# First attention's q and o weight gradients moved into the lead of the backward sweep, with other moves of loads, tiles and tick order

## The chip, the cores and the metric

The kernel runs on one core of a Trainium2 chip. The metric is the device time of one execution in microseconds (us). Several executions are timed, and their median is the time of a kernel. One execution more is recorded by the profiler; it has a time of its own.

## The reference

Inputs are x of 2048 tokens by 576, weights of two attentions, a gate vector and an output gradient, all bf16. The reference computes a forward pass and the gradient of everything in it:

```python
def _fwd_reference(...):                       # x is A_x; out = g*a + (1-g)*b
    g = _sigmoid((x * gate_w).sum(-1, keepdims=True))
    # A: 32 query heads of 18, one key and value head
    q = (x @ wq) as (32, 2048, 18); k = x @ wk; v = x @ wv
    a = softmax(q k^T * 18 ** -0.5) v, heads joined, @ wo
    # B: 64 segments of 32 tokens, one after the other, 32 heads of 128
    mem = mem0                                 # 8 rows
    for s in range(64):
        h = concatenate([mem, B_x of segment s])       # 40 rows
        q, k, v = h Wq, h Wk, h Wv
        p = softmax(q k^T * 128 ** -0.5, causal among the 32, memory always seen)
        o = (p v) Wo
        mem = o[:8]; outs.append(o[8:])
    b = concatenate(outs)
# returned: the output, and by jax.vjp the gradients of x, wq, wk, wv, wo,
# mem0, Wq, Wk, Wv, Wo and gate_w
```

In the kernel's list of outputs, outs[2] is the gradient of wq (x^T times dq) and outs[5] that of wo (o^T times da, where da is the gradient that reaches attention A's output and o its heads before wo). Both are sums over 2048 tokens of a 576 by 576 product.

## The kernel before, in words

Attention A and attention B share the core. B's memory makes its 64 segments a chain, forward and backward, whose steps are short and wait for each other. So the kernel runs each chain as a generator and weaves into it, step by step, another generator with A's work, which has no chain: `weave` (line 279) takes one step of the sweep per step of the chain. The stages are, in order, with their times in the profiled execution:

1. Preparation, the projections of B for all tokens, weights kept on chip or stored (0 to 440 us).
2. `b_chain_fwd` (line 333), B's forward chain over 64 segments, woven with `a_pass1`, A's forward and query-side backward pass (440 to 2135). In each segment a chain step makes q, k and v of the memory rows. `rows_copy` copies their rows and `rows_out` stores them, both through POOL's queue; `expand` (line 267) spreads probabilities over blocks on POOL.
3. `b_bulk` (line 658), the attention of B's tokens, forward and backward, for all segments (2137 to 2782). It is a software pipeline written out by hand: 16 token tiles of 8 groups of 4 heads are 128 units, and 137 ticks run over them. In each tick the list `order` says which stages are issued and how many units back each one works. `st_QT`, `st_KT`, `st_VT`, `st_GT` and `st_OT` transpose a tile on PE into a PSUM tile x_tr, of which there are two, and DVE or ACT copies it out. QT and KT carry a ride, the transposes of dS and P (x_DT and x_PT). `st_SDm` and `st_SDx` make the scores and their gradient, `st_M` masks, `st_R` sums and divides (DVE, then POOL's x_P), `st_Om` and `st_Ox` make the output, `st_Qm` and `st_Qx` the query gradient, `st_K` the memory's key and value gradients, and `B_(i)` the output projection. An engine executes its instructions in the order in which they are issued here.
4. `b_chain_bwd` (line 993), B's backward chain over 64 segments of 14 steps, woven with `a_pass2` (line 1863), the key-side sweep of A (2782 to 4388). One sweep step (the "unit") makes scores, exponentials (b_E, ACT), probabilities' gradients (b_dS, DVE) and the two accumulations for 512 columns. Its queries come in pieces of 800 columns (b_QS), one for four steps, and its keys as b_KV. SWEEP of 1024 units run here, the rest in stage 6. Twelve steps of the sweep lead, and `extra` puts 22 more into the chain's first segment.
5. `b_post` (line 1272): gradients that the chain left for later (4388 to 4604).
6. `b_dw` (line 1401): B's weight gradients, woven with the rest of the sweep, one unit for every WCOLS columns of matmul; six units come first (4604 to 5373).
7. `a_final` (line 1992): A's input gradient f_dx and A's weight gradients (5373 to the end).

Three weight tiles WT0, WT1, WT2 of 4.7 MB each (`alloc_WT`) and the output weights WoT of 4.7 MB are stored in stage 1 and 2 and loaded again for the backward chain: WT by `load_WT` in 12 pieces on SP's queue, at every fourth step from the lead's first (WT2, then WT0, then WT1), WoT by `load_WoT` on POOL's queue. Pools of SBUF are stacked: a pool opened later lies behind an earlier one, and where its tiles lie over tiles of the stage before, their first writers wait for the last readers there. Within `b_chain_bwd` the pools are rw (WoT), a3s, a3k (sweep), rs and rk, rv, rd (chain).

In stage 7 the sums for outs[2] and outs[5] are ten groups of 16 steps over token tiles, each step a matmul of 512 columns and one of 64 (PSUM tile f_big). Each group leaves through a copy f_o and a store on SP. Their operands ot and da come by `final_tok` (line 1965) at the end of stage 6.

Of the kernel before, what the change touches and what calls it, by code (L numbers as in the profile page):

```python
# [12 lines left out]
BF16 = mybir.dt.bfloat16  # L13
F32 = mybir.dt.float32
U16 = mybir.dt.uint16
U32 = mybir.dt.uint32
P = 128

D = 576
NKT = 5  # L20
# [13 lines left out]
KT_ROWS = [128, 128, 128, 128, 64]  # L34
# [1 line left out]
KR = 9  # L36
KVT = 11
KV4 = 9
SWEEP = 928
QSW = 800  # L40
WCOLS = 13312
RIDE = 24


# [6 lines left out]
class Kern:  # L51
# [224 lines left out]
    def m_rows(self, t, c):  # L276
        return t[32 * c:32 * c + 8].rearrange("p u e -> p (u e)")

    def weave(self, chain, sweep, lead, extra=(), early=None, n_early=0):
        steps = itertools.count()  # L280

        def step():
            i = next(steps)
            if i % 4 == 0 and i // 4 < n_early:
                early(i // 4)
            next(sweep, None)

        for _ in range(lead):
            step()
        extra = dict(extra)  # L290
        for i, _ in enumerate(chain):
            for _ in range(1 + extra.get(i, 0)):
                step()
        for _ in sweep:
            pass
# [37 lines left out]
    def b_chain_fwd(self, keep, sp, psum):  # L333
        nc = self.nc
# [68 lines left out]
        for s in range(NSEG):  # L403
# [79 lines left out]
            qT = sp.tile([P, 8, 4, 8], BF16, name="c_qT", bufs=1)  # L483
            nc.scalar.copy(qT[:], src)
            mT_store("k")
            rows_copy("k")
            rows_out("q")
            if s < 48:
                stash_end(*wt)
# [30 lines left out]
            proj("v", 1, (0, 1))  # L520
            yield
            proj("v", 1, (2, 3, 4))
            rows_copy("q")
            yield
            po = psum.tile([P, 8, 64], F32, name="c_x", bufs=1)
# [2 lines left out]
            for u in range(8):  # L528
                self.mm(po[:, u, 0:32], lhsT=vx[:, u, :], rhs=PBx[:, u].rearrange("p c q -> p (c q)"),
                        start=False, stop=True)  # L530
# [107 lines left out]
    def alloc_WoT(self, pool):  # L638
        self.WoT = (pool.tile([P, 4, J], BF16, name="WoT"), pool.tile([P, 4, 512], BF16, name="WoTt"))

    def load_WoT(self, pool):
        self.alloc_WoT(pool)
        for kt in range(4):
            self.nc.gpsimd.dma_start(self.WoT[0][:, kt, :], self.st_WoT[kt])
        self.nc.gpsimd.dma_start(self.WoT[1][:], self.st_WoTt[:])

    def load_blockdiag(self, t, src, tt):
        for i in range(4):
# [9 lines left out]
    def b_bulk(self, wp, lp, sp, psum):  # L658
# [243 lines left out]
        def st_K(t):  # L902
# [12 lines left out]
            if t % 4 == 3:  # L915
                c2 = t // 4 % 2
                for i in range(4):
# [1 line left out]
                    due[1].append((dst[i][:, 4 * c2:4 * c2 + 4, :], dm[32 * i:32 * i + 32].rearrange("p g w e -> p g (w e)")))  # L919

        B_ = lambda i: lambda t: st_B(t, i)
        order = [(None, st_QT), (7, B_(0)), (None, st_KT), (7, B_(1)), (4, st_Om), (5, st_OT), (7, B_(2)), (5, st_VT),
                 (7, B_(3)), (None, st_SDm), (0, st_GT), (9, st_Qm), (2, st_R), (7, st_K),
                 (None, st_SDx), (1, st_M), (4, st_Ox), (9, st_Qx)]
        done = {st_Ox: (4,), st_VT: (5,), st_SDx: (6,), st_K: (7,), st_Qx: (9,)}
        for names in (deep, ("mT", "v", "vB", "kB")):
            load(0, names)
# [62 lines left out]
        v = lambda t: t.rearrange("p (c u) d -> p c (u d)", u=8)[:, :, u * D:(u + 2) * D]  # L990
        self.nc.sync.dma_start(v(self.WT[wi][:]), v(self.st_WT[wi]))

    def b_chain_bwd(self, wot, sp, kd, kvp, keep, psum):
        nc = self.nc
        NSEG, T = self.NSEG, self.T
        self.load_WoT(wot)
        dm = [keep.tile([P, NSL, 32], BF16, name=f"dm{i}") for i in range(2)]
        hs = keep.tile([P, 2, GD], BF16, name="r_hs")
        hx = keep.tile([P, 2, 16], BF16, name="r_hx")
# [272 lines left out]
    def b_post(self, sp, rp, psum, wH):  # L1272
# [4 lines left out]
        NG = NTT * 8  # L1277
        NC = NG // 2
        pdx, C, sB, mR, T_ = {}, {}, {}, {}, {}

        def load_s(n):
            tt = NTT - 1 - n
# [10 lines left out]
        def load(c, names):  # L1293
            if c >= NC:
                return
            tt, h0 = NTT - 1 - c // 4, 8 * (c % 4)
            d = C.setdefault(c, {})
            if tt >= self.NTT - KVT:
                names = [{"q": "dk", "dO": "dv"}.get(w, w) for w in names if w != "pd"]
            for w in names:  # L1300
                if w in ("dk", "dv"):
                    d[w] = sp.tile([P, 8, P], BF16, name=f"y_l{w}", bufs=3)
                    nc.sync.dma_start(d[w][:].rearrange("p h e -> p (h e)"),
                                      self.xtok[w][tt * P:(tt + 1) * P, h0 * P:h0 * P + 1024])
                    continue
                if w == "pd":
                    d[w] = rp.tile([P, 2, 8, SEG], BF16, name="y_pd", bufs=3)
                    nc.sync.dma_start(d[w][:], self.pd_dram[tt][:, :, h0:h0 + 8, :])
                    continue
                d[w] = (rp if w == "q" else sp).tile([P, 8, P], BF16, name=f"y_{w}", bufs=3)  # L1310
                if w == "dq":
                    nc.sync.dma_start_transpose(d[w][:], self.xtok[w][tt * P:(tt + 1) * P, h0 * P:h0 * P + 1024])
                else:
                    nc.sync.dma_start(d[w][:].rearrange("p h e -> p (h e)"),
                                      self.xtok[w][tt * P:(tt + 1) * P, h0 * P:h0 * P + 1024])

        def st_KV(t):
            tt, g, r, d = NTT - 1 - t // 8, t % 8, slice(4 * (t % 2), 4 * (t % 2) + 4), C[t // 2]
            if tt >= self.NTT - KVT:
                return  # L1320
            pks = []
            for x in (1, 0):
                pk = psum.tile([P, 4, P], F32, name="y_pk", bufs=2)
                c, h2 = slice(32 * (g // 2), 32 * (g // 2) + 32), g % 2
                for i in range(4):
                    self.mm(pk[:, i, :], lhsT=sB[tt][c, i, h2, x, :], rhs=mR[tt][c, x, 4 * h2 + i, :],
                            start=True, stop=False, tp=(c.start, 0))
                pks.append(pk)
            for x, pk in zip((1, 0), pks):
                self.diag_mm(pk, d["pd"][:, x, r], d["q" if x else "dO"][:, r])  # L1330
            for w, pk in zip(("dk", "dv"), pks):
                if t % 2 == 0:
                    d[w] = sp.tile([P, 8, P], BF16, name=f"y_t{w}", bufs=2)
                nc.scalar.copy(d[w][:, r, :], pk[:])
                if t % 2 == 1:
                    h0 = 8 * (t // 2 % 4)
                    nc.gpsimd.dma_start(self.xtok[w][tt * P:(tt + 1) * P, h0 * P:h0 * P + 1024],
                                      d[w][:].rearrange("p h e -> p (h e)"))

        def st_T(t):  # L1340
            d = C[t // 2]
            T_[t] = {"dq": d["dq"][:, 4 * (t % 2):4 * (t % 2) + 4, :]}
            for w in ("dk", "dv"):
                pt = psum.tile([P, 4, P], BF16, name="y_pt", bufs=2)
                for i in range(4):
                    self.tr(pt[:, i, :], d[w][:, 4 * (t % 2) + i, :], P)
                T_[t][w] = sp.tile([P, 4, P], BF16, name="y_T", bufs=5)
                nc.vector.tensor_copy(T_[t][w][:], pt[:])
            if t % 2 == 1:
                C.pop(t // 2)  # L1350
# [15 lines left out]
                nc.gpsimd.dma_start(self.dxB_dram[tt * P:tt * P + n, :], dx[0:n, :])  # L1366

        stages = (st_KV, st_T, st_H)
        dxt = [sp.tile([P, D], BF16, name=f"y_dx{i}") for i in range(2)]
        load(0, ("pd", "q", "dO"))  # L1370
        load(0, ("dq",))
        load_s(0)
# [7 lines left out]
        for t in range(NG + len(stages) - 1):  # L1380
            if t % 3 == 2 and 0 <= t - 11 < 30:
                next(hist[(t - 11) // 15])
            if t == 16:
                for g in range(2):
                    nc.gpsimd.dma_start(
                        self.dxB_dram[T0:self.T, 288 * g:288 * g + 288].rearrange("(s r) c -> s r c", r=RIDE),
                        self.dxr_dram[0:self.NSEG - KR, 32 * g:32 * g + RIDE, :])
            for n, st in enumerate(stages):
                if 0 <= t - n < NG:
                    st(t - n)  # L1390
                if n == 0 and t == 31:
                    self.ht = self.load_h(self.db_dram, self.dm_dram, wH)
                if n == 0 and t < NG:
                    if t % 2 == 1:
                        load(t // 2 + 3, ("pd", "q", "dO"))
                    if t % 8 == 7:
                        load_s(t // 8 + 2)
                if n == 1 and t % 2 == 0 and t >= 2:
                    load(t // 2 + 2, ("dq",))

    def b_dw(self, sp, wA, wB, wH, psum, sweep):
        nc = self.nc
# [69 lines left out]
        with self.tc.manual_schedule():  # L1472
# [37 lines left out]
                nc.vector.tensor_copy(dg16[0:1, hf, :], pg[hf][0:1, 0:288])  # L1510
            nc.sync.dma_start(self.outs[11][None, :], dg16[0:1].rearrange("p a b -> p (a b)"))
            self.ftok["x"] = ht
            self.final_tok(wB, ("ot", "da"))

    def setup_A_dram(self, dram):
        T = self.T
# [475 lines left out]
    def a_final(self, sp, psum):  # L1992
# [37 lines left out]
        for kt in range(NKT):  # L2030
            drows = KT_ROWS[kt]
            cs = slice(kt * P, kt * P + drows)
            for (l, r, o) in (("x", "dq", 2), ("ot", "da", 5)):
                pw = psum.tile([P, 640], F32, name="f_big", bufs=2)
                self.row_mm(pw[0:drows], [(tok[l][:, tt, cs], tok[r][:, tt, :]) for tt in range(NTT)])
                o16 = sp.tile([P, D], BF16, name="f_o16", bufs=2)
                self.evac(o16[0:drows, :], pw[0:drows, 0:D])
                nc.sync.dma_start(self.outs[o][cs, :], o16[0:drows, :])
            pk = psum.tile([P, 4, 36], F32, name="f_pk", bufs=1)
            for tt in range(NTT):  # L2040
                self.mm(pk[0:drows, 0, :], lhsT=tok["x"][:, tt, cs], rhs=dkt[:, tt, :], start=(tt == 0),
# [7 lines left out]
def build_full(tc, A_x, A_wq, A_wk, A_wv, A_wo, B_mem0, B_Wq, B_Wk, B_Wv, B_Wo, gate_w, grad_out, outs_raw,  # L2049
# [10 lines left out]
    with SB("const") as cpool, tc.tile_pool(name="dram", bufs=1, space=bass.MemoryType.DRAM) as dram:  # L2060
# [18 lines left out]
        with ExitStack() as man:  # L2079
# [37 lines left out]
            tw = ExitStack()  # L2117
            twp = tw.enter_context(SB("tw"))
            k.alloc_WT(twp)
            with SB("rw") as rw, SB("a3s") as a3s, SB("a3k") as a3k, SB("rs") as rs, \  # L2120
                    SB("rk") as rk, SB("rv") as rv, SB("rd") as rd, PS("rp") as rp, PS("a3p") as a3p:
                k.weave(k.b_chain_bwd(rw, rs, rd, rv, rk, rp), k.a_pass2(a3k, a3s, a3p, 0, SWEEP, nc.sync, rv, 3), 12,
                        {4: 8, 7: 6, 9: 8}, k.load_WT, 12)
            wHs = ExitStack()
            wH = wHs.enter_context(SB("wH", RIGHT))
            with SB("yr", RIGHT) as yr, SB("ys") as ys, PS("yp") as yp:
# [83 lines left out]
```

## Time and profile before

| what | us |
|---|---|
| median of 3 executions | 5443.15 |
| lowest and highest | 5434.64 to 5444.33 |
| profiled execution, its time | 5478.13 |
| profiled execution, its span | 5476.4 |
| lead and first segment of the backward chain | 2782 to 2881 |
| first of the ten groups for outs[2] and outs[5] | 5424.52 |
| last DMA issue | 5465.6 |

The profile's engines are PE (matmul), PEld (its weight load, beside matmuls), DVE, ACT, POOL and SP, whose queue issues DMAs. In a row of the timeline come start, length, engine, source line, operation, output and inputs with their shapes, the count, and in brackets how long the engine was idle before and what ended that. In a row of the chain come start, length and what ran. In a row of waits: engine, who ended the wait, total us, how often, the longest. L86 is the helper through which all matmuls are issued and L91 the one for transposes, so rows are told apart by tile names. The mean granted clock of PE over the span was 0.981.

### The profile page before, as it was taken

The page shows a single profiled execution, that of the slowest core. Times are in us where ns is not written, and L with a number is a line of the kernel's source. Part 1 is how long each engine was busy: PE and PEld are TensorE (multiplying, and loading weights), DVE is VectorE, ACT ScalarE, POOL GpSimd, SP SyncE. Part 2 cuts the span into 40 slices and gives each one's busy share as a digit, 9 for nine tenths or more (in the row PEclk, how much of TensorE's full clock was granted, in tenths as well). Part 3 has the DMA queues.
Part 4 walks back from the last instruction along what each step waited for, and adds up shares of the span by engine and source line. Part 5 has one row for each costly group of instructions (what it writes and reads, how often), then busy time and mean ns, then how long its engine had stood idle before and what let it go on. Part 6 is the DMA issues. An engine that isn't in the chain of part 4 may idle for free. (4 is left out here: it accounts for less than half of the span.)

```text
span 5476.4 us, 221351 instructions
## 1 busy us (share of the span) xinstructions
PE 5171.7 (94%) x95713; PEld 2805.1 (51%) x95713; DVE 3579.9 (65%) x7083; ACT 3306.7 (60%) x4738; POOL 2163.2 (40%) x4186
## 2 busy tenths in 40 slices
PE   7999999999999998999979999999999998999998
PEld 6434444444444444766635555555555476754444
DVE  5337888888888887666658778888788822333322
ACT  4327787777777886655557777777777722222211
POOL 4004554555555544433324455455445411121113
PEclk9999999999999999999979999999999999999999
DMA  6645776666676555888874788888888878956553
GB/s 216 222 173 130 138 138 130 131 135 130 133 134 121 112 111 144 259 250 248 255 243 128 184 181 184 181 185 183 180 184 184 160 201 213 255 187 205 182 165 108
DMA packets 1048630, 959.14 MB, mean 175 GB/s; under 512 B 598882, under 2 KB 896747, under 8 KB 1038050
## 3 DMA queue, kind: packets, MB, share of 16 engines
q1 hardware_dynamic: 938434, 687.66, 54.2%
q0 software_dynamic: 100784, 247.24, 14.8%
q8 instruction: 748, 12.26, 1.0%
q10 hardware_dynamic: 8432, 10.08, 0.6%
q14 instruction: 232, 1.90, 0.1%
HBM read 522.08 MB, written 371.33 MB: 163 GB/s over the span
## 5 line engine op out<-in xcount | busy, mean ns | idle before, releaser
L1918 DVE TENSOR_TENSOR b_dS<-b_dP,b_E 128x512 bf16<-128x512 f32 x2048 | 1315.4, 684 | 533.5 <-PE b_dP L86 246.0
L1779 DVE TENSOR_TENSOR a_W<-a_dP,a_E 128x512 bf16<-128x512 f32 x2048 | 1315.7, 685 | 288.0 <-issue 131.3
L1893 ACT ACTIVATE b_E<-b_S 128x1024 bf16<-128x1024 f32 x1024 | 1048.8, 1024 | 605.2 <-PE b_dP L86 505.4
L1749 ACT ACTIVATE a_E<-a_S 128x1024 bf16<-128x1024 f32 x1024 | 1049.9, 1025 | 260.9 <-PE a_dP L86 173.4
L86 PEld LDWEIGHTS <-b_QS 32*128 32x128 bf16 (+1 forms) x8192 | 235.5, 89 | 564.0 <-issue 512.3
L86 PE MATMUL b_S<-b_KV,b_QS 32*128 32x512 bf16 x2048 | 408.7, 392 | 91.5 <-ACT b_E L1893 67.3
L86 PE MATMUL r_pj<-WT,r_dT 128*32 128x288 bf16 x12288 | 488.6, 289 | 6.0 <-issue 5.8
L86 PE MATMUL w_acc<-w_d,w_h 128*128 128x512 bf16 (+1 forms) x2400 | 484.6, 380 | 0.0
L86 PE MATMUL a_S<-a_QD,l_KV 32*128 32x512 bf16 x2048 | 400.6, 385 | 38.0 <-ACT a_E L1749 33.2
L86 PE MATMUL b_acc<-b_dS,b_QS 128*18 128x512 bf16 x2048 | 420.5, 392 | 3.2 <-issue 2.4
L86 PE MATMUL a_acc<-a_W,l_WK 128*32 128x512 bf16 x4096 | 413.8, 391 | 0.3 <-DVE a_W L1779 0.2
L86 PE MATMUL a_acc<-a_E,l_VK 128*32 128x512 bf16 x4096 | 404.7, 381 | 7.2 <-issue 2.7
L86 PE MATMUL b_dP<-b_KV,b_QS 32*128 32x512 bf16 x2048 | 409.2, 394 | 1.3 <-DVE b_dS L1918 1.3
L86 PE MATMUL b_acc<-b_E,b_QS 128*18 128x512 bf16 x2048 | 405.9, 392 | 2.1 <-issue 2.1
L86 PE MATMUL a_dP<-a_QD,l_KV 32*128 32x512 bf16 x2048 | 399.7, 386 | 0.5 <-issue 0.5
L86 PEld LDWEIGHTS <-r_dT 128*32 128x32 bf16 x12288 | 323.9, 97 | 101.2 <-issue 13.8
L86 PEld LDWEIGHTS <-w_h 128*128 128x128 bf16 (+1 forms) x2688 | 224.9, 100 | 257.9 <-issue 20.9
L86 PEld LDWEIGHTS <-hm 128*32 128x32 bf16 x7680 | 203.7, 97 | 195.7 <-issue 1.4
L870 POOL TENSOR_TENSOR x_prod<-x_dOT,x_oT 128x512 bf16<-128x512 bf16 x128 | 148.0, 1157 | 296.8 <-ACT x_oT L867 274.2
L86 PEld LDWEIGHTS <-l_KV 32*128 32x128 bf16 x4096 | 121.6, 91 | 250.1 <-issue 205.5
L86 PEld LDWEIGHTS <-l_WK 128*32 128x32 bf16 x4096 | 106.7, 93 | 222.0 <-issue 221.7
L86 PE MATMUL x_b<-WoN,x_oT 128*128 128x288 bf16 x1024 | 212.6, 291 | 3.2 <-issue 3.2
(465 smaller groups left out, 10106.7 us busy)
## 6 DMA issues: line engine op xcount, KB each, us to landing
b_QS<-qs_dram SPq DMA_DIRECT2D x232, 200.0 KB
dOx_dram<-p_tok SPq DMA_DIRECT2D x16, 1024.0 KB
c_vx<-vx_dram SPq DMA_DIRECT2D x64, 256.0 KB
krow_dram<-c_k POOLq DMA_DIRECT2D x64, 256.0 KB, 5.2
qrow_dram<-c_q POOLq DMA_DIRECT2D x64, 256.0 KB, 3.9
vrow_dram<-c_v POOLq DMA_DIRECT2D x64, 256.0 KB
x_q<-qx_dram SPq DMA_DIRECT2D x32, 512.0 KB
x_dO<-dOx_dram SPq DMA_DIRECT2D x32, 512.0 KB
```

The lines of the kernel that those rows point to most:

```text
L86: return self.nc.tensor.matmul(out, lhsT, rhs, start=start, stop=stop, tile_position=tp, skip_group_check=True)
L870: nc.gpsimd.tensor_tensor(out=sc["prod", t][:], in0=sc["dOT", t][:], in1=oT[:], op=ALU.mult)
L1749: nc.scalar.activation(E_[n][:], S.pop(n)[:], ACT.Exp, scale=SCALEA)
L1779: nc.vector.tensor_tensor(out=W_[n][:, i, :], in0=dP[i][:], in1=E_[n][:, i, :], op=ALU.mult)
L1893: nc.scalar.activation(E_[n][:], S.pop(n)[:], ACT.Exp, scale=SCALEA)
L1918: nc.vector.tensor_tensor(out=D_[n][:, i, :], in0=dP[i][:], in1=E_[n][:, i, :], op=ALU.mult)
```

## The change

- SWEEP goes from 928 to 936 and WCOLS from 13312 to 14592; the 22 extra sweep steps in the first segment go, and the lead is 40 steps instead of 12 (PRE + 32).
- The ten groups and the load of ot and da leave stage 7 and the end of stage 6. The new generator `lead_dw` makes the same sums in the last 32 steps of the lead, ten matmuls of 288 columns a step, in the chain's PSUM banks r_pj and r_x; ACT copies and POOL stores each result. Its operands are loaded into WT0 and WT1 at the lead's first step, by `early_bwd`.
- `early_bwd` also sets the loads of the weights by step: WT2 at steps 3, 5, 7, 9; WoT at 11 to 19, now on SP; WT0 at 25 to 31; WT1 at 41 to 47. `weave` calls it behind the sweep's step and no longer ahead of it.
- The pools of the backward chain are stacked in another order, so that the sweep's tiles lie elsewhere.
- In `b_bulk` the list `order` is another one, of the same stages with the same distances.
- In `b_chain_fwd` the copies of the key rows are issued later, next to those of the query rows.
- In `b_post` five kinds of tiles become fixed tiles taken in turn, and the load of dq is issued at another stage, at odd units.

```diff
-SWEEP = 928
+SWEEP = 936
-WCOLS = 13312
+WCOLS = 14592
+PRE = 8
...
-    def weave(self, chain, sweep, lead, extra=(), early=None, n_early=0):
+    def weave(self, chain, sweep, lead, extra=(), early=None, pre=None):
...
-            if i % 4 == 0 and i // 4 < n_early:
-                early(i // 4)
             next(sweep, None)
+            if early is not None:
+                early(i)
+            if pre is not None and i >= PRE:
+                next(pre, None)
...
             mT_store("k")
-            rows_copy("k")
             rows_out("q")
...
             proj("v", 1, (2, 3, 4))
+            rows_copy("k")
             rows_copy("q")
...
-    def load_WoT(self, pool):
-        self.alloc_WoT(pool)
-        for kt in range(4):
-            self.nc.gpsimd.dma_start(self.WoT[0][:, kt, :], self.st_WoT[kt])
-        self.nc.gpsimd.dma_start(self.WoT[1][:], self.st_WoTt[:])
+    def load_WoT(self, kt):
+        if kt < 4:
+            self.nc.sync.dma_start(self.WoT[0][:, kt, :], self.st_WoT[kt])
+        else:
+            self.nc.sync.dma_start(self.WoT[1][:], self.st_WoTt[:])
+
+    def early_bwd(self, i):
+        ld = self.nc.sync.dma_start
+        if i == 0:
+            v = lambda d: d[:, 0:D].rearrange("(n p) d -> p n d", p=P)
+            ld(self.WT[0][:, 16:32, :], v(self.dqtok_dram))
+            ld(self.WT[0][:, 0:16, :], v(self.A_x))
+            ld(self.WT[1][:, 0:16, :], v(self.otok_dram))
+            ld(self.WT[1][:, 16:32, :], v(self.da_dram))
+        for k in range(4):
+            if i == 3 + 2 * k:
+                self.load_WT(k)
+            if i == PRE + 17 + 2 * k:
+                self.load_WT(4 + k)
+            if i == PRE + 33 + 2 * k:
+                self.load_WT(8 + k)
+        if i in (11, 13, 15, 17, 19):
+            self.load_WoT((i - 11) // 2)
+
+    def lead_dw(self, kvp, psum):
+        nc = self.nc
+        units = [(self.WT[w], o, kt, hf) for w, o in ((0, 2), (1, 5)) for kt in range(NKT) for hf in range(2)]
+        n, out = 0, None
+        for u, (t, o, kt, hf) in enumerate(units):
+            rows = KT_ROWS[kt]
+            pw = psum.tile([P, 512], F32, name=("r_pj", "r_x")[u % 2], bufs=1)
+            for tt in range(self.NTT):
+                self.mm(pw[0:rows, 0:288], lhsT=t[:, tt, kt * P:kt * P + rows],
+                        rhs=t[:, 16 + tt, 288 * hf:288 * hf + 288], start=(tt == 0), stop=(tt == self.NTT - 1))
+                n += 1
+                if n % 10 == 0:
+                    yield
...
+            def out(pw=pw, o=o, kt=kt, hf=hf, rows=rows):
...
+                nc.scalar.copy(f, pw[0:rows, 0:288])
+                nc.gpsimd.dma_start(self.outs[o][kt * P:kt * P + rows, 288 * hf:288 * hf + 288], f)
...
-        order = [(None, st_QT), (7, B_(0)), (None, st_KT), (7, B_(1)), (4, st_Om), (5, st_OT), (7, B_(2)), (5, st_VT),
-                 (7, B_(3)), (None, st_SDm), (0, st_GT), (9, st_Qm), (2, st_R), (7, st_K),
-                 (None, st_SDx), (1, st_M), (4, st_Ox), (9, st_Qx)]
+        order = [(4, st_Om), (4, st_Ox), (2, st_R), (None, st_QT), (7, B_(0)), (9, st_Qm), (9, st_Qx), (None, st_KT),
+                 (7, B_(1)), (5, st_OT), (7, B_(2)), (None, st_SDm), (5, st_VT), (7, B_(3)), (0, st_GT), (7, st_K),
+                 (None, st_SDx), (1, st_M)]
...
+        dxt = [sp.tile([P, D], BF16, name=f"y_dx{i}") for i in range(2)]
+        turn = {w: itertools.cycle([sp.tile([P, h, P], BF16, name=f"y_{w}{i}") for i in range(n)])
+                for w, h, n in (("T", 4, 5), ("dq", 8, 3), ("tdk", 8, 2), ("tdv", 8, 2), ("dO", 8, 3))}
...
-                if n == 1 and t % 2 == 0 and t >= 2:
-                    load(t // 2 + 2, ("dq",))
+                if n == 2 and t % 2 == 1 and t >= 3:
+                    load((t + 3) // 2, ("dq",))
...
-            self.final_tok(wB, ("ot", "da"))
...
-            for (l, r, o) in (("x", "dq", 2), ("ot", "da", 5)):
-                pw = psum.tile([P, 640], F32, name="f_big", bufs=2)
-                self.row_mm(pw[0:drows], [(tok[l][:, tt, cs], tok[r][:, tt, :]) for tt in range(NTT)])
-                o16 = sp.tile([P, D], BF16, name="f_o16", bufs=2)
-                self.evac(o16[0:drows, :], pw[0:drows, 0:D])
-                nc.sync.dma_start(self.outs[o][cs, :], o16[0:drows, :])
...
-            with SB("rw") as rw, SB("a3s") as a3s, SB("a3k") as a3k, SB("rs") as rs, \
+            with SB("rw") as rw, SB("rs") as rs, SB("a3k") as a3k, SB("a3s") as a3s, \
                     SB("rk") as rk, SB("rv") as rv, SB("rd") as rd, PS("rp") as rp, PS("a3p") as a3p:
-                k.weave(k.b_chain_bwd(rw, rs, rd, rv, rk, rp), k.a_pass2(a3k, a3s, a3p, 0, SWEEP, nc.sync, rv, 3), 12,
-                        {4: 8, 7: 6, 9: 8}, k.load_WT, 12)
+                k.alloc_WoT(rw)
+                k.weave(k.b_chain_bwd(rs, rd, rv, rk, rp), k.a_pass2(a3k, a3s, a3p, 0, SWEEP, nc.sync, rv, 3), PRE + 32,
+                        (), k.early_bwd, k.lead_dw(rv, rp))
```

More of the change, by code (lines that the diff above doesn't have):

```diff
@@ new lines, in lead_dw @@
+    def lead_dw(self, kvp, psum):
[11 more added lines that the diff above has]
+                    yield
+                    if out is not None:
+                        out()
+                        out = None
+            def out(pw=pw, o=o, kt=kt, hf=hf, rows=rows):
+                o16 = kvp.tile([P, 4, P], BF16, name="r_kvo", bufs=2)
+                f = o16[0:rows].rearrange("p a b -> p (a b)")[:, 0:288]
+                nc.scalar.copy(f, pw[0:rows, 0:288])
+                nc.gpsimd.dma_start(self.outs[o][kt * P:kt * P + rows, 288 * hf:288 * hf + 288], f)
+        out()
@@ L991, in load_WT, with b_chain_bwd @@
         self.nc.sync.dma_start(v(self.WT[wi][:]), v(self.st_WT[wi]))
-    def b_chain_bwd(self, wot, sp, kd, kvp, keep, psum):
+    def b_chain_bwd(self, sp, kd, kvp, keep, psum):
         nc = self.nc
         NSEG, T = self.NSEG, self.T
-        self.load_WoT(wot)
         dm = [keep.tile([P, NSL, 32], BF16, name=f"dm{i}") for i in range(2)]
@@ L1309, in load @@
                     continue
-                d[w] = (rp if w == "q" else sp).tile([P, 8, P], BF16, name=f"y_{w}", bufs=3)
+                d[w] = rp.tile([P, 8, P], BF16, name="y_q", bufs=3) if w == "q" else next(turn[w])
                 if w == "dq":
@@ L1332, in st_KV @@
                 if t % 2 == 0:
-                    d[w] = sp.tile([P, 8, P], BF16, name=f"y_t{w}", bufs=2)
+                    d[w] = next(turn["t" + w])
                 nc.scalar.copy(d[w][:, r, :], pk[:])
@@ L1346, in st_T @@
                     self.tr(pt[:, i, :], d[w][:, 4 * (t % 2) + i, :], P)
-                T_[t][w] = sp.tile([P, 4, P], BF16, name="y_T", bufs=5)
+                T_[t][w] = next(turn["T"])
                 nc.vector.tensor_copy(T_[t][w][:], pt[:])
@@ L1368, in b_post @@
         stages = (st_KV, st_T, st_H)
-        dxt = [sp.tile([P, D], BF16, name=f"y_dx{i}") for i in range(2)]
         load(0, ("pd", "q", "dO"))
```

## The prediction

> **What bounds the kernel now.** I read the page first, then the chain that ended last, then the timeline and the table of stretches around the edges between stages, and last the waits inside the bulk stage. The page says that PE is the engine to spare:
>
> ```profile
> PE 5171.7 (94%) x95713; PEld 2805.1 (51%) x95713; DVE 3579.9 (65%) x7083; ACT 3306.7 (60%) x4738; POOL 2163.2 (40%) x4186
> ```
>
> The idle 6% lies at edges and in the bulk, so a change gains where it takes PE work out of a stretch that only PE fills, or puts work where PE idles. The chain (start, length, what) shows the places that this change touches:
>
> ```profile
> 4529.72 11.57 DMA y_dO<-dOx_dram
> ...
> 4548.21 4.68 DMA y_dO<-dOx_dram
> ...
> 4598.65 5.89 PE y_pdx L86 x48
> 4604.62 16.15 DMA w_d<-ox_dram
> ...
> 4633.25 6.70 DMA z_src<-dTm_dram
> ...
> 5420.74 43.34 PE f_big L86 x344
> ```
>
> The last row is the kernel's end: 344 matmuls in a row with nothing beside them. 320 of them are the ten q and o gradient groups. The timeline has the groups' starts, and the two places where PE waits for the first key-side queries:
>
> ```profile
> 2782.86 0.59 SPq L991 DMA_DIRECT2D WT<-st_WT  x1
> 2783.55 0.59 SPq L1871 DMA_DIRECT2D b_KV<-kv_dram  x1
> ...
> 2792.25 0.61 PE L86 MATMUL b_S<-b_KV,b_QS 32*128 32x512 bf16 x2 [9.61 <-DMA b_QS<-qs_dram]
> ```
> ```profile
> 4612.99 0.61 PE L86 MATMUL b_S<-b_KV,b_QS 32*128 32x512 bf16 x2 [8.46 <-DMA b_QS<-qs_dram]
> ```
> ```profile
> 5424.52 4.08 PE L86 MATMUL f_big<-w_d,w_h 128*128 128x512 bf16 x32
> ...
> 5428.44 4.08 PE L86 MATMUL f_big<-w_d 128*128 128x512 bf16 x32
> ```
>
> The stretches (length, busy time of the five engines, granted clock, DMA share, GB/s) show the lead of the backward sweep, 2792 to 2815, at half clock with PE not full, and the end with DVE, ACT and POOL empty:
>
> ```profile
> 2800.00:2815.00 15.00, 9.54 (x68) 2.41 (x64) 11.18 (x18) 9.05 (x9) 0.24 (x1) 0.50 0.91 342
> 2815.00:2820.00 5.00, 4.40 (x52) 1.34 (x52) 4.57 (x11) 1.63 (x3) 1.16 (x2) 0.63 0.42 115
> 2820.00:2840.00 20.00, 13.62 (x217) 5.57 (x221) 15.51 (x26) 13.29 (x15) 5.29 (x10) 0.72 0.90 305
> 5424.00:5466.00 42.00, 40.58 (x343) 21.72 (x343) 4.59 (x6) 3.37 (x6) 4.46 (x6) 1.00 0.12 41
> ```
>
> In the bulk stage (2150 to 2760) PE's weight loads wait for DVE to empty the transposes' bank, twice in most ticks:
>
> ```profile
> PEld L91 <- DVE x_PT L754: 31.6, 107, 0.4
> PEld L91 <- DVE x_DT L754: 27.7, 90, 0.5
> PEld L91 <- issue: 16.5, 19, 4.4
> PEld L91 <- POOL x_P L847: 9.3, 12, 5.2
> ```
>
> **The change part by part.** The sum is made against the profiled run (5478.13 us, span 5476.4). That run is 35 us, 0.64%, above the median of 5443.15, so I carry over the difference and not the time. About 0.2%, 11 us, is what a measurement here can tell from no change.
>
> *The end.* The ten groups start at 5424.52 and 5428.44, so 3.92 us each, 39.2 us in all. Without them the last issue is no longer the 5465.63 one of the chain but the POOL store of f_dx at 5428.10; the tail of 10.8 us behind it stays: -37.5. The two operand loads (2 x 2304 KB) and ten stores leave too; they sit beside the 2.6 us chain of out_dram<-f_dx waits ahead of 5420, and I take -2 (0 to -5).
>
> *The lead.* Before, it and the first chain segment run from PE's last bulk work at 2782.6 to 2880.8. They hold 12 lead steps, 14 chain steps and 22 extra steps, 48 sweep steps. After, there are 40 + 14 = 54, and 320 matmuls of 288 columns. Step by step:
> - Start. The new pool order lets b_KV and three b_QS be issued before the bulk ends, ahead of the weight loads. The wait of 9.61 goes; the first exponential then waits for ACT's last x_dq copies. Start 2785.
> - Eight steps alone at half clock. Steps start 1.76 us apart in the stretch before 2815: 14 us, to 2799. By then the first two operands must be in: 0.75 MB of key-side data and 4.72 MB at 342 GB/s is 16 us from 2783.5, 2799.5. Just covered.
> - 32 steps with ten gradient matmuls. A 288-column matmul at full clock is 2.94/24 = 0.1225 us (y_pdx rows of the chain) or 5.89/48, so 1.225 a step. A sweep step in the weight-gradient stage costs PE 0.81 (its 26-matmul period is 6.37 us there, less 26 x 0.2135). Sum 2.04 us, more than the 1.55 at which such steps follow each other at full clock with chain work between, so PE sets the pace and ACT copies (20 x 0.40) and stores hide.
> - A stall. The fourth b_QS is queued on SP behind all four operand loads, 9.44 MB. In all 10.4 MB at 342 GB/s is 30.4 us: it lands at 2814. Sweep step 11 reaches it at about 2806 (three mixed steps, the first at half clock). PE is in order, so gradient matmuls behind that step wait too: 8 us. That a small load waits out a large one on this queue is what 11.57 against 4.68 for the same y_dO load shows; the former was issued behind a 2304 KB w_h load. Then 29 x 2.04 = 59, and 2 for the clock to rise: 2875.
> - First segment without extras, 14 steps, 23 us as in later segments: 2898 against 2880.8. **+17**, between +7 (no stall, no second rise) and +27 (weights, now queued on SP too, late at the first segment).
>
> The same SP queue now carries the output weights that POOL's queue carried. WT2 and WoT, 9.2 MB by step 19, take 27 us at 342 GB/s while 16 steps take 33, so later b_QS loads keep up.
>
> The Trainium skill ("DMA: Bandwidth & Descriptors", section Bandwidth) gives 425 GB/s for a 16 MB transfer, where the trace has 342. By it the stall would be about 2 us and the time 6 us less.
>
> *Eight fewer sweep units in the weight-gradient stage.* Their share there is 0.81 each: -6.5. The wider spacing lets 88 units cover what 96 covered.
>
> *Edge from b_post to b_dw.* The first w_d load leaves SP when the last st_KV is done (last y_pk at 4593.9) instead of after the last y_pdx at 4604.62. Its 2 MB move while DMA is 0.10 busy (4590 to 4605), and so no longer beside the b_QS loads, which stay behind ACT's last y_dx copy: 8.46 falls to perhaps 4.5 (-4). SP runs ten us ahead, so z_src, issued at 4633.25 and landing at 4639.95, is there in time: PE's waits of 3.64 and 1.35 for z_v go (-5). **-9** (-3 to -13). The fixed y_ tiles and the later dq load cost nothing: three buffers still hold it two ticks ahead.
>
> *Forward chain.* POOL waits 106.9 us (35 times) for krow_dram<-c_k with rows_out behind it, but PE waits for POOL's c_PBm only 9.5 us. Moving the key copies behind the products: -3 (-10 to +3; its DMA issues now precede the query copies).
>
> *Bulk order.* 137 ticks of 4.5 us. R (0.41 + 0.18 on DVE) moves ahead of QT's copy. The transposes of OT wait for x_DT, so they are 0.59 later; Qm and Qx (0.78) come between QT and KT and Om (0.38) leaves, which covers 0.40: that wait goes from 0.31 to 0.50. SDm (0.8) comes between OT and VT, which covers VT's wait for x_PT (0.30) whole. Net -0.1 a tick: **-13**. Bounds: all of 27.7 + 31.6 gone, -59; R's 0.59 uncovered for half the ticks, +40. I stay near the walk.
>
> Sum: -37.5 - 2 + 17 - 6.5 - 9 - 3 - 13 = -54. Profiled run 5424; median 5443 - 54 = **5389**.
>
> **The rivals.**
> - *The bulk's new order costs.* R now stands ahead of every QT copy on DVE, the next bank is not free, and a stall opens at each tick. For it: both waits today are DVE's, and DVE is 63% busy there. Against: the covers above. Without the bulk the sum is -41, so it decides from 41/137 = 0.30 us a tick. At 0.5 a tick it is +68 - 41 = +27: 5470, slower. Chance 0.11.
> - *The bulk's waits go altogether.* -59 for -13: 5343. The row for x_PT speaks for half of it (-30: 5372). Chance 0.15.
> - *The lead stays at a low clock.* From 2820 to 2840 the grant was 0.72 although PE was at work 13.6 of 20 us. At 0.67, 32 x 2.04 us become 97: +32, 5421. Against: 0.50 rose to 1.00 by 2820 behind dense r_pj work. Chance 0.09. The Trainium skill ("TensorE: Matmul & The Clock Gate", Part 1) has full speed after about 3.4 us of sustained activity, which speaks against this rival; the 0.72 row does not show when mixed work counts as such.
> - *SP's queue sets the lead.* Between step 0 and the end of the first segment SP carries 9.44 MB of operands, 18.8 MB of weights and some 3 MB of b_QS. At 342 GB/s these 31 MB take 91 us from 2783.5, to 2875, just when the lead ends; at 250 they take 125, so 2909, and with the last weights' use behind it the segment ends near 2920: +22, 5411. For it: 208 GB/s between 2840 and 2880 in the table of stretches. Against: DMA share was only 0.65 there, so demand set that rate. Chance 0.12.
> - *The forecast*, with or without the stall (5379 to 5399): 0.53.
>
> **How the numbers follow.** 5389 is the likeliest case. The range takes in, below, the bulk at half its waits (-17), no stall (-10) and ten for the lower ends of the smaller terms: 5352. Above, it takes in the bulk at +0.2 a tick (+40) and a lead longer by 14: 5443. Faster: the forecast, the waits gone, and most of the low clock and of the queue, 0.84. Same, the bulk's mild losses: 0.06. Slower, the bulk rival: 0.10.
>
> **What would show it.** After the last f_dx store nothing but the tail, f_big ending near the end minus 12 us. In the lead: PE's first b_S 2 to 3 us after the bulk's last matmul, a wait of 3 to 10 us for b_QS after the eleventh step, steps 2.0 apart at clock 1.00, sweep plus first segment taking about 116 us from the bulk's end against 98. In b_dw the waits for z_v gone. In the bulk the x_PT wait near zero, x_DT's longer, and the stage 646 to 632 us. The prediction is wrong if the bulk is longer by over 40 us or the lead with its first segment takes over 145.

## The result, and the profile after

The changed kernel takes 5427.42 us (median of 20 executions, 5406.01 to 5449.72) against 5442.15 for the kernel before (20 executions, 5434.64 to 5453.12). The ratio is 0.9972, 95% interval 0.9962 to 0.9981: 15 us faster, with 10 to 21 inside the interval. The forecast was 54 us. The sign was right, and the size was not.

The two profiled executions differ by 50.6 us in span (5476.4 and 5425.8), which looks like the forecast and is not. The profiled execution of before, 5478.13, lies above all 20 timed ones. So I had the kernel before profiled again (b_again below) and read stages from both. Stage times, from the first and last instruction of their tiles on PE (the forward chain by c_pj, b_post by y_pdx):

| stage, us | before | before again | after |
|---|---|---|---|
| forward chain | 1700.2 | 1686.5 | 1679.6 |
| bulk, first x_q transpose to last x_po | 636.0 | 623.6 | 645.6 |
| bulk's end to the end of the first backward segment | 98.3 | 98.8 | 130.1 |
| the other 63 segments | 1507.0 | 1500.6 | 1495.6 |
| b_post | 213.9 | 213.1 | 213.1 |
| b_post's end to the first w_acc | 20.5 | 20.7 | 16.4 |
| first to last w_acc | 752.6 | 749.1 | 740.8 |
| a_final on PE | 84.9 | 86.6 | 42.8 |
| tail behind it | 11.8 | 11.8 | 7.9 |

Now the lines of after that answer those of before. PE's share of the page has hardly moved, since the same matmuls are made:

```profile
PE 5179.5 (95%) x95713; PEld 2809.5 (52%) x95713; DVE 3579.4 (66%) x7078; ACT 3336.6 (61%) x4753; POOL 2177.1 (40%) x4201
```

The chain that ended last, its last pieces. The 43.34 us of matmul are gone, and it ends with f_dx and two small stores:

```profile
5413.35 2.08 PE f_big L87 x12
...
5416.42 1.27 POOL f_dx L2073
...
5421.77 0.56 POOL out_dram L2085
```

PE in the timeline of the lead, and at the edge to b_dw. The first key-side matmul now follows the bulk at once, but the next waits 4.02 us for ACT, whose last bulk copies come behind DMA issues. The fourth b_QS stalls PE by 7.65 us, and the last weights by 5.76. At the edge to b_dw 8.46 has become 4.36:

```profile
2773.04 0.39 PE L87 MATMUL b_S<-b_KV,b_QS 32*128 32x512 bf16 x2
2777.45 0.61 PE L87 MATMUL b_S<-b_KV,b_QS 32*128 32x512 bf16 x2 [4.02 <-ACT b_E L1938]
...
2807.67 0.60 PE L87 MATMUL b_S<-b_KV,b_QS 32*128 32x512 bf16 x2 [7.65 <-DMA b_QS<-qs_dram]
...
2900.74 1.15 PE L87 MATMUL r_pj<-WT,r_dT 128*32 128x288 bf16 x16 [5.76 <-DMA WT<-st_WT]
```
```profile
4620.14 0.61 PE L87 MATMUL b_S<-b_KV,b_QS 32*128 32x512 bf16 x2 [4.36 <-DMA b_QS<-qs_dram]
```

The stretches (columns as before): the stall stands in the row from 2800, with PE busy 7.35 of 15 us and the DMA engines full; after it PE is full at clock 1.00.

```profile
2785.00:2800.00 15.00, 12.29 (x86) 4.91 (x82) 9.02 (x14) 7.46 (x8) 0.00 (x0) 0.61 1.08 355
2800.00:2815.00 15.00, 7.35 (x45) 3.18 (x44) 2.64 (x5) 2.44 (x4) 1.16 (x2) 0.66 1.07 378
2815.00:2840.00 25.00, 24.68 (x224) 13.89 (x221) 16.00 (x25) 14.85 (x20) 3.80 (x7) 1.00 0.80 307
5417.00:5426.00 9.00, 0.91 (x19) 0.72 (x18) 0.81 (x1) 0.18 (x1) 3.65 (x5) 0.76 0.10 33
```

The bulk's waits (2121 to 2772). x_PT's 31.6 us are gone, x_DT's are as before, a smaller one for x_dOT is new. By these rows the stage should be shorter, and it is longer:

```profile
PEld L92 <- DVE x_DT L799: 26.7, 96, 0.8
PEld L87 <- DVE x_dOT L813: 14.0, 60, 0.4
...
PEld L92 <- DVE x_PT L800: 0.8, 1, 0.8
```

What the waits do not show stands in the starts of PE's matmuls in one tick, first of after, then of before:

```profile
2502.36 0.34 PE L87 MATMUL x_SD<-x_vT,x_dOT 128*32 128x32 bf16 x16
2502.63 0.39 PE L87 MATMUL x_po<-x_vmB,x_PT 128*128 128x512 bf16 x1
2502.95 0.40 PE L87 MATMUL x_po<-x_v,x_PT 32*32 32x128 bf16 x16
2503.28 0.40 PE L92 MATMUL x_tr<-identB,x_q 128*128 128x128 bf16 x4
```
```profile
2505.54 0.26 PE L86 MATMUL x_SD<-x_vT,x_dOT 128*32 128x32 bf16 x16
2505.73 0.40 PE L86 MATMUL x_po<-x_v,x_PT 32*32 32x128 bf16 x16
2505.97 0.39 PE L86 MATMUL x_po<-x_k,x_DT 32*32 32x128 bf16 x16
2506.29 0.40 PE L91 MATMUL x_tr<-identB,x_q 128*128 128x128 bf16 x4
```

The shape ahead of the columns (128*128, 128*32, 32*32) is the part of the array that a matmul uses. In before, Ox and Qx, both 32*32, follow each other 0.24 us apart. In after Ox stands alone: Om streams 512 columns, 0.213 us, yet Ox starts 0.32 behind it, and x_q starts 0.33 behind Ox, where in before Qx followed Ox by 0.24. Each change of shape leaves about 0.1 us in which nothing streams. I took the 80 or so undisturbed ticks of each trace (3.9 to 4.95 us long) and, from the distance between the starts of two consecutive matmuls, subtracted the time of the first one's columns, at 0.2135 us for 512 as in the weight-gradient stage. Before: three changes a tick, 0.092, 0.096 and 0.091 us. After: six, 0.106, 0.097, 0.096, 0.093, 0.093 and 0.096. That is +0.30 a tick. The transposes' wait ahead of VT falls from 0.149 to nothing, that ahead of OT rises from 0.066 to 0.130. Together these are +0.22 a tick; the mean undisturbed tick rose by 0.17, from 4.373 to 4.545, so the other gaps must have shrunk by some 0.05. Of all ticks, disturbed ones too, the middle one takes 4.63 us in each of five profiles with the new list and 4.51 in each of five with the list of before: 0.12 to 0.13 longer, 16 us over 127 ticks.

### The profile page after: what moved, and what is told of

Its sections match the earlier page's. It is cut to its first block, busy times and chain, and to the rows that moved or that the text cites. A ratio compares the mean times of both kernels' runs of the same rounds, so it can differ in the third digit from the quotient of the medians.

```text
span 5425.8 us, 221553 instructions
## 1 busy us (share of the span) xinstructions
PE 5179.5 (95%) x95713; PEld 2809.5 (52%) x95713; DVE 3579.4 (66%) x7078; ACT 3336.6 (61%) x4753; POOL 2177.1 (40%) x4201
```

## The experiments

Names that begin with b_ start from the kernel before, those with a_ from the changed one.

**b_again**, the kernel before as it is.

> The kernel before, unchanged, profiled a second time. The profiled execution of before was 35 us over its own median; its forward chain took 1700.2 us and that of the changed kernel 1679.6. If the 20.6 us are an effect of the later key copies, the forward chain takes 1695 to 1705 again. If they belong to that one execution, it takes 1680 to 1690. In the bulk stage, undisturbed ticks should again be 4.37 us in the mean, because they are PE's own sequence.

Span 5443.0. Forward chain 1686.5, as expected if the length belonged to the one execution, and undisturbed ticks of 4.43, a little over the expected 4.37. The first profile of before was 13.7 us longer in the forward chain and 12.4 in the bulk. A forward chain that long is not the first profile's alone: b_noqo's took 1698.9.

**a_oldorder**, the bulk list of before in the changed kernel.

```diff
-        order = [(4, st_Om), (4, st_Ox), (2, st_R), (None, st_QT), ... ]
+        order = [(None, st_QT), (7, B_(0)), (None, st_KT), (7, B_(1)), (4, st_Om), ... ]   # as before
```

> The changed kernel with the list of bulk stages of the kernel before. Theory (the new order costs about 0.17 us in each undisturbed tick): undisturbed ticks go from 4.55 back to 4.37 us, the bulk stage is shorter by 10 to 25 us, and the median falls from 5427 to 5405 - 5417. Rival (the bulk's 9.6 us between the two profiles are chance): ticks the same as in the changed kernel, median within 5 us of it.

Ticks 4.375, median 5409.35, ratio to before 0.9939 (0.9920 to 0.9957). The new list costs some 18 us of the whole; its interval does not meet that of the changed kernel, if by little. In the one profile, an execution 9 us over the median, the stage takes 640.2 us, only 5 less than in the changed kernel, where 10 to 25 were expected. The wait for x_PT is back in its trace:

```profile
PEld L92 <- DVE x_PT L799: 32.1, 107, 0.4
```

**a_ends**, new list, Ox and Qx behind SDx.

```diff
-        order = [(4, st_Om), (4, st_Ox), (2, st_R), ... (9, st_Qm), (9, st_Qx), ... (1, st_M)]
+        order = [(4, st_Om), (2, st_R), ... (9, st_Qm), ... (1, st_M), (4, st_Ox), (9, st_Qx)]
```

> The changed kernel with its new order, but with Ox and Qx put back, side by side, behind SDx and M at the end of the tick. Theory (in the new order each block of 32x32 matmuls follows a block on the full array and starts some 0.2 us late, once for Ox and once for Qx, while the wait for x_PT is gone): undisturbed ticks fall to 4.15 - 4.25 us, below both kernels, and the median to 5385 - 5410. Rival (the loss has another place in the new order, such as R ahead of QT): ticks stay at 4.45 or more, median 5415 to 5430.

Ticks 4.65, median 5426.75 (ratio 0.9971, 0.9957 to 0.9984): by these numbers the rival's side. But the run separates nothing, because I had made a new wait. Of x_po there are two PSUM tiles; with Ox and Qx at the end of one tick and Om at the head of the next, Om waits for ACT to empty one (PE's waits in the bulk):

```profile
PE x_po L87 <- ACT x_o L785: 65.5, 114, 2.5
```

Ahead of Ox there is one change of 0.092 us again and none ahead of Qx, and both waits for x_DT and x_PT are gone. It says why such lists put Om and Ox side by side, and does not decide on the theory.

**a_b0mid**, B0 between Om and Ox.

```diff
-        order = [(4, st_Om), (4, st_Ox), (2, st_R), (None, st_QT), (7, B_(0)), ...
+        order = [(4, st_Om), (7, B_(0)), (4, st_Ox), (2, st_R), (None, st_QT), ...
```

> The changed kernel with one output projection, B0, moved between Om and Ox, all else as changed. If Ox starts late because it adds to the PSUM tile that Om has just written, B0 fills that time and undisturbed ticks fall by 0.2 to about 4.35 us. If it starts late because the array changes from full-height matmuls to 32x32 ones, it starts late behind B0 as well, and ticks stay at 4.5 to 4.6.

Ticks 4.552, Ox 0.104 late behind B0 as it was 0.106 late behind Om. So it is not the PSUM tile, it is the shape.

**a_sdm**, the old list with SDm between B2 and VT.

```diff
-        ... (5, st_OT), (7, B_(2)), (5, st_VT), (7, B_(3)), (None, st_SDm), (0, st_GT), ...
+        ... (5, st_OT), (7, B_(2)), (None, st_SDm), (5, st_VT), (7, B_(3)), (0, st_GT), ...
```

> The changed kernel with the old list of bulk stages, but with SDm moved from behind B3 to ahead of VT, so that it covers the transposes' wait for x_PT. Theory (each change of the array's shape costs 0.095 us, the old list has three a tick and the new one six, and what the new list gains is the x_PT wait alone): three changes and no x_PT wait, so undisturbed ticks of 4.373 - 0.149 = 4.22 us, 0.32 below the changed kernel and 0.15 below the old list; the median 10 to 20 us below the 5409 of the old list. Rival (the wait for x_PT went because R came early, not because of SDm's cover): ticks 4.37, median 5405 to 5415.

The wait for x_PT is gone without R being early, and changes stay at three: ticks 4.274, 0.10 below the old list where 0.15 was expected. But more ticks are disturbed (37 over 5.2 us, 28 with the old list), the stage takes 639.6 us against 640.2, and the median of 5410.84 (ratio 0.9948, 0.9932 to 0.9964) is that of a_oldorder, not the 10 to 20 us less that were expected. In this profile the 13 us that shorter ticks should give stand against longer disturbed ones. That need not be the list's doing: in a_best the same list has 29 such ticks and a stage of 629.3 us. What disturbs them stays open.

**a_nostall**, staging loads spread over the lead (the edit in short).

```diff
-        if i == 0: ... ld(WT[1] <- otok), ld(WT[1] <- da)     # WT2 at 3..9, WoT at 11..19, WT0 at 25..31
+        if i == 4: ld(WT[1] <- otok)
+        if i == 6: ld(WT[1] <- da)                            # WT2 at 10..16, WoT at 18..26, WT0 at 28..34
```

> The changed kernel with its staging loads spread out: operands of the o gradient at steps 4 and 6 and no longer at step 0, WT2 at 10 to 16, WoT at 18 to 26, WT0 at 28 to 34. Theory (the fourth b_QS stands behind 9.4 MB on SP's queue): the wait of 7.7 us for b_QS goes, the lead falls from 98.5 to about 90 us, the time by 6 to 9 us. Rival (the lead is bound by the bytes as a whole, so a stall only comes later): the lead stays within 3 us of 98.5, with waits at later b_QS.

No wait for b_QS, lead 86.0 us instead of 98.5 (93.7 to 98.5 in the six profiles with the changed kernel's lead), median 5410.85 (ratio 0.9950, 0.9936 to 0.9963). More than the stall's own 7.65 came back, and more than the 6 to 9 expected. The stretch that held the stall is full, at full clock:

```profile
2800.00:2815.00 15.00, 14.67 (x134) 8.04 (x131) 9.62 (x15) 8.92 (x12) 2.22 (x5) 1.00 1.07 380
```

**a_nodw**, without the lead's 320 matmuls, their copies and stores, so that outs[2] and outs[5] are not made.

```diff
-                self.mm(pw[0:rows, 0:288], lhsT=t[:, tt, ...], rhs=t[:, 16 + tt, ...], ...)
                 n += 1
...
-                nc.scalar.copy(f, pw[0:rows, 0:288])
-                nc.gpsimd.dma_start(self.outs[o][...], f)
```

> The changed kernel with the 320 gradient matmuls of the lead, their copies and stores left out (outs[2] and outs[5] are not made); their operand loads, all 40 lead steps and the order of everything else stay. The lead's length, 98.5 us with them, says what 39.2 us of matmul cost there. If the work fills idle PE time: 82 to 90 us (34 us until the fourth b_QS has landed, then 29 steps at 1.76), so a price of 9 to 16. If it is paid in full: 60 us.

Lead 86.4 us. So 39.2 us of matmul cost 7 to 12 there by those six profiles. The stall that the loads make is in both, 11.5 us here and 7.65 in the changed kernel's, so outside it they cost some 4 more.

**b_noqo**, the kernel before without the ten groups at the end and their loads, so that outs[2] and outs[5] are not made.

```diff
-            self.final_tok(wB, ("ot", "da"))
...
-            for (l, r, o) in (("x", "dq", 2), ("ot", "da", 5)):
...
-                nc.sync.dma_start(self.outs[o][cs, :], o16[0:drows, :])
```

> The kernel before with the ten q and o gradient groups and their loads at the end left out (outs[2] and outs[5] are not made). It prices the end alone. Forecast's term: 37.5 + 2 = 39.5 us less. From the changed kernel's profile, where the end stage and its tail are shorter by 43.8 + 3.9: 44 to 48 less, a median of 5393 to 5403.

Median 5404.0, ratio 0.9927 (0.9909 to 0.9944), so 40 us (30 to 49) of that day's 5439.17; the two medians differ by 35. That is nearer the forecast's 39.5 than the 44 to 48 of the stages.

**a_undo**, the headline part alone undone (the edit in short).

```diff
-SWEEP = 936, WCOLS = 14592; lead PRE + 32; lead_dw; early_bwd by steps
+SWEEP = 928, WCOLS = 13312; lead 12, extra {4: 8, 7: 6, 9: 8}; WoT on POOL's queue; groups back in a_final
```

> The changed kernel with its headline part alone undone: the q and o gradients are made at the end again, the lead is 12 steps, the 22 extra steps are back, SWEEP 928 and WCOLS 13312, weights loaded at every fourth step and WoT by POOL's queue. Pool order, bulk list, key copies and post tiles stay as changed. By the stages of the profiles the headline part gives 44 + 4 us at the end and 6.5 in the weight-gradient stage and takes 130.1 - (98.3 - 9.6) = 41 us in lead and first segment: undone, the median rises by some 13 us to 5435 - 5447. Rival (the lead hides nothing and the whole gain comes from the other parts): within 5 us of 5427. Rival of the forecast (the lead takes 17 + 9.6 us only): 5450 or more.

Median 5436.32, ratio 0.9992 (0.9978 to 1.0006): the headline part is worth about 9 us by the medians, 13 were expected. The interval just meets that of the changed kernel (0.9962 to 0.9981), so it may be worth nothing. One thing was off: lead and first segment took 99.6 us, as in before, although the start's wait of 9.6 was gone. The 9.6 came back as ACT's 4.4 at the start, and 1.2, 1.4, 1.5 and 1.5 for WoT, its tail, r_dx and dm, and in steps at half clock:

```profile
2782.42 0.61 PE L87 MATMUL b_S<-b_KV,b_QS 32*128 32x512 bf16 x2 [4.42 <-ACT b_E L1930]
2807.10 0.62 PE L87 MATMUL r_pj<-WoT,dm 128*32 128x512 bf16 x4 [1.21 <-DMA WoT<-st_WoT]
2809.14 0.62 PE L87 MATMUL r_pj<-WoTt,dm 128*32 128x512 bf16 x4 [1.42 <-DMA WoTt<-st_WoTt]
```

**a_fwdold** and **b_fwdnew**, the place of the key copies alone.

```diff
 # b_fwdnew; a_fwdold is the reverse in the changed kernel
-            rows_copy("k")          # ahead of rows_out("q")
+            rows_copy("k")          # ahead of rows_copy("q")
```

> The changed kernel with the copies of the key rows where they were before. Two profiles of the kernel before gave 1700.2 and 1686.5 us for the forward chain, four with later key copies 1673 to 1680. If the copies' place does it: forward chain of 1686 us or more, POOL's waits for krow_dram back at about 100 us, median 5 to 15 us above the changed kernel. If it is chance: 1673 to 1682 and a median within 5 us.

> The kernel before with only the copies of the key rows issued later. Three profiles of the forward chain with the early copies in the kernel before gave 1686 to 1700 us; one with early copies in the changed kernel gave 1674.9; eight with later copies 1673 to 1682. If the copies' place is worth time: forward chain 1673 to 1683, median 8 to 18 us below before (ratio 0.9967 to 0.9985). If the difference comes from something else in the changed program: forward chain 1686 or more, and a ratio within 0.001 of one.

a_fwdold: forward chain 1674.9 in its profile, median 5433.44 (ratio 0.9986, 0.9975 to 0.9996). b_fwdnew: forward chain 1676.0, median 5440.84, ratio 1.0009 (0.9996 to 1.0022). POOL's waits for krow_dram go with the later copies (68.7 us in a_fwdold, none in the changed kernel), and the time does not follow: the two medians speak against each other, and the forward chain of a single profile varies by more than the effect. I count it as nothing that can be told.

**a_best**, a_sdm's list, a_nostall's loads, and WT1 at steps 40 to 43.

```diff
-            if i == PRE + 33 + 2 * k:
+            if i == PRE + 32 + k:
                 self.load_WT(8 + k)
```

> The changed kernel with three repairs: bulk list as in a_sdm, staging loads spread as in a_nostall, WT1 loaded at steps 40, 41, 42, 43 and no longer 41 to 47. If the terms add: 17 us from the list, 12 from the lead, 3 to 6 from the wait for WT1, so 5427 - 32 = 5395 (5385 to 5405). If they share a cause in the loads, no better than either alone, 5405 to 5412.

Median 5397.72, ratio 0.9915 (0.9897 to 0.9934): 44 us faster than before and 30 faster than the changed kernel, as expected if the terms add. List and loads alone gave 17 each, so these two nearly add. The third repair shows no gain. The wait for WT1, 3.4 us in a_nostall, is gone, but in the same segment PE now waits 4.20 us for DVE:

```profile
2869.38 0.58 PE L87 MATMUL b_dP<-b_KV,b_QS 32*128 32x512 bf16 x1 [4.20 <-DVE b_dS L1965]
```

DVE waited for POOL, and POOL 8.19 us for a small load of the next segment (r_pT), which SP had issued behind the four pieces of WT1. Lead and first segment take 118.2 us, 117.2 in a_nostall.

## Why the prediction was off, step by step

**The bulk order: -13 forecast, about +17 measured.** This is the step that failed. The cover for x_PT did what the walk said: its wait fell from 31.6 to 0.8 us. The waits were sized too large, since the rows are of PEld, which runs beside PE: in PE's starts the wait ahead of VT was 0.149 a tick and not 0.30, and that ahead of OT rose by 0.064 and not 0.19. But their sum, -0.09 a tick, is near the walk's -0.1, which is luck; and the rival that had both waits go altogether at -59 could have had 0.149 + 0.066 a tick, some 27 us. What failed is that the walk took a matmul block to cost the same wherever it stands, and so put changes of shape at nothing. Pulling Om with Ox, and Qm with Qx, together tore Ox from Qx, and three more changes of shape at 0.095 us, +0.30 a tick, outweigh what the waits gave. Five profiles with the new list, and a_b0mid's, gave 641 to 648 us for the stage, four of kernels before with their list 624 to 636; a_oldorder has 18 us by medians. The old list in the changed kernel's one profile took 640.2, so the size rests on the medians and the ticks, and how much of the stage's growth beyond them is chance stays open. The rival on the other side had the sign and the place and the wrong mechanism: it laid the loss to DVE, which in fact made PE wait less.

**The lead: +17 forecast, +31 measured** (27 to 32 in the six profiles with that lead). The structure was right, down to the stall: forecast from 23 to 31 us behind the bulk's end, it ran from 27 to 35, 7.65 us for 8. By the 425 GB/s of the Trainium skill ("DMA: Bandwidth & Descriptors", section Bandwidth) the stall would have been an estimated 2 us; the trace had 355 to 378 GB/s from 2785 to 2815, nearer the 342 of the row. Three terms were too small and make up the 14.7 us. The fourth b_QS, which ends the stall, came 3.2 us later than forecast. The dense steps take 63.8 us and not 61 with the rise of the clock: (2871.5 - 2807.7)/29 = 2.20 us and not 2.04, with 3.6 us of PE's waits for ACT's copies of the gradients (r_kvo) that I had called hidden. The first segment takes 31.7 and not 23: 5.76 of it is the wait for WT1, which I had only as an upper bound, and the first segment of before already took 65.3 - 22 x 1.76 = 26.6 without its extra steps (31.2 at the 1.55 of full clock). And the wait of 9.6 at the start was no gain of 8: ACT's 4.02 followed it, and a_undo shows that without the new lead all of it turns into later waits.

**The end: -39.5 forecast.** 40 by b_noqo. In the profile 43.8 less on PE, against b_again, and 3.9 less behind it.

**Units and edge: -6.5 and -9 forecast.** Against before's two profiles the edge gave 4.1 to 4.3 and the weight-gradient stage 8.3 to 11.8, 12 to 16 of 15.5. The parts are as forecast: 8.46 to 4.36 at the edge, and the two waits for z_v gone.

**Forward chain: -3 forecast**, nothing that can be told.

Summed with what was measured: -44 - 4 + 31 - 14 + 17 = -14, against -15 by the medians. The agreement is partly luck: with b_noqo's 40 for the end the sum is -6, and the other 63 segments, 5 to 11 us shorter, and the forward chain stand in neither sum. The low-clock rival fell: the grant is 1.00 from 2815 on, and b_S's length falls from 0.60 to 0.39 us by 2798, five us after dense work began; the Trainium skill ("TensorE: Matmul & The Clock Gate", Part 1) has about 3.4. The stall brought half clock back for 2804 to 2814. The rival of SP's queue was right in kind: a_nostall shows that the order of that queue, not its bytes, held 8 to 12 us of the lead, and a_best that moving WT1 up in it only moves the wait.

## What to carry to other kernels

Count shape changes before reordering PE's work: matmuls that use the same part of the array belong side by side, and a row of waits does not show what a change costs. When work moves into a stretch with idle time, its loads move too: lay them out by the step that needs each, since a small load behind large ones on the same queue stalls everything behind it in PE's order. And take stage times from more than one profile before explaining a difference: here one profiled execution lay 35 us above the median.

## What the runs showed of the hardware

A change between 128*128, 128*32 and 32*32 matmuls cost PE 0.091 to 0.107 us each, in the undisturbed ticks of all six traces that I read for it, whichever way it went and whatever PSUM tile was written. The Trainium skill ("TensorEngine Tiling (Array Packing)", section Key Properties) says that a change of tiling mode drains the engine, with which these gaps agree; I had not brought it to the bulk's list, where it spoke against the change. The first of the four operand loads kept SP for 0.38 us; with it in the queue, each of the next four issues, the other three operand loads and the fourth b_QS, kept SP itself for 4.4 to 7.2 us:

```profile
2775.13 4.41 SPq L655 DMA_DIRECT2D WT<-in_A_x_dram  x1
2779.65 6.78 SPq L656 DMA_DIRECT2D WT<-otok_dram  x1
2786.47 6.46 SPq L657 DMA_DIRECT2D WT<-da_dram  x1
2793.05 7.23 SPq L1924 DMA_DIRECT2D b_QS<-qs_dram  x1
```

So the fourth b_QS left SP only at about 2800, and a wait for a load can begin in the queue of its issuer.
